# An attention block and a gated feed-forward layer on one core: another order of the loading phase, and the scores of the first two batches transposed together

## The chip, the cores and the metric

The kernel runs on one core of one Trainium2 chip. The time is the device time of one execution in microseconds (us); a run's time is compared with runs of the kernel before on the same chip. TensorE is called PE here, VectorE DVE, ScalarE ACT, GpSimd POOL, and SyncE, which only issues transfers here, SP.

## What is computed

```python
# x (8, 8, 512, 64), state (8, 8, 32, 64), both fp32; D = 64, scale = 1/8
scores  = scale * x @ state.T ;  a  = softmax(scores)   # 512 rows of 32
xread   = a @ state
scores2 = scale * state @ x.T ;  a2 = softmax(scores2)  # 32 rows of 512
sread   = a2 @ x
y = concat([xread, sread], axis=2)       # per batch 512 + 32 rows, 8 heads x 64 = 512 wide
gate = sigmoid(y @ w_gate);  val = y @ w_val            # 512 x 1536 each
out  = (gate * val) @ w_out                             # 1536 x 512 -> (4352, 512) fp32
```

## The kernel before

For the 512 x-rows of a batch, `xread @ W` is never formed from `xread`. The kernel first multiplies the state with both weight matrices (`sw_visit`, `sw_wide`: two PSUM tiles, one for each parity e of the head, copied to the SBUF tile `SW` by `sw_cp`), and then `SW` with the transposed probabilities `aT` (`gv_mm(b, f)`: four matmuls of 512 columns, two for the gate, two for the value, for block f of 12). ACT takes a tanh of the gate half (`gv_th`), DVE multiplies it with the value half (`gv_glu`), and `out_mm(b, k)` (four matmuls) is one third of one of four output tiles; after the last third ACT copies the tile (`res`) and SP writes it.

The probabilities of a batch b come from `S_mm` (halves i = 0, 1), `S_max` and `S_sub` (DVE), `S_exp` (ACT), `n_sum` (DVE, a reduction and a reciprocal), `n_mul` (POOL), and a transposition: `aT_mm` with `aT_cp` on PE, ACT and DVE for batches 0 and 1, `aT_dma` (SP) for the others. The second softmax, by columns, is `cT_mm` (scores transposed, one PSUM tile for each e), `cT_max` (DVE), `cT_exp` (ACT), `cT_nrm` (a reciprocal `rc` on DVE, then `cN` on POOL), `c_dma` (SP transposes), and `sr_mm` with `sr_cp` (the 32 rows of `sread`, put into `XS`). All eight batches' `XS` rows go through the feed-forward layer together as "batch 8" at the end.

The order on each engine is the order of the program's lines (`manual_schedule`): an instruction that waits holds up all that stand behind it on its engine. PSUM has eight tiles of one bank: two named GV, four SWP, one OU, one AT; the caller names the place. A tile can be used again when all that read its last content are through. SBUF pools have rings too; the one that matters is `cE` (output of `cT_exp`) with two buffers, which POOL's `cN` reads.

The program has three parts: a loading phase and prologue, written out as a list of calls (L423 to L694), in which batches 0 and 1 are computed as far as their weights have landed and batch 2 is prepared; a loop over b = 2 to 8 and f = 0 to 11 (L696), in which block f of batch b stands beside a third of an output tile of batch b - 1 and the preparation of batch b + 1 (`row`, `col`); and a tail. The second softmax of batches 0 and 1 is left to the stage b = 7, which prepares no batch. There `col(0, f)` runs in f = 0 to 4 and `col(1, f - 3)` in f = 3 to 7. In that stage the order in each f is a third of an output tile of batch 6, block f of batch 7, and then these steps.

Weights come by POOL's queue in column blocks of 256 or 512 (`load_w(w, lo, n)`, w = 0 gate, 1 value), x by SP's queue (batch 2's and 3's by POOL's), the state by both; `gate(...)` is a one-column POOL copy that makes POOL wait for something before it issues more. `warm(n, place)` is n small matmuls of ones whose result is not used; before and after have 87 of them in all.

Of the kernel before, what the change touches and what calls it, by code (L numbers as in the profile page):

```python
# [10 lines left out]
AF = mybir.ActivationFunctionType  # L11
# [5 lines left out]
def kernel(  # L17
# [14 lines left out]
    nc = tc.nc  # L32
# [311 lines left out]
    def warm(n, place):  # L344

        ps = place[0].tile((128, 512), FP, name="warm", tag=place[1])
        for _ in range(n):
            nc.tensor.matmul(ps[:, :128], ones[:, 0], ones[:, 0], start=True, stop=True)  # L348
# [36 lines left out]
    def col(b, t):  # L385
# [11 lines left out]
        else:  # L397
            cT_nrm(b, 1, nc.gpsimd)
            c_dma(b)

    def row(b, t):

        if t == 0:
            S_mm(b, 0, AT)
            S_max(b, 0)
        elif t == 1:
            S_sub(b, 0)
            S_mm(b, 1, SWP)
            S_max(b, 1)
        elif t == 2:  # L410
            S_sub(b, 1)
            S_exp(b, 0)
        elif t == 3:
            S_exp(b, 1)
            n_sum(b, 0)
            n_mul(b, 0, nc.gpsimd)
        elif t == 4:
            n_sum(b, 1)
            n_mul(b, 1, nc.gpsimd)
        else:  # L420
            aT_dma(b)
# [7 lines left out]
        nc.vector.memset(ones[:, e, 64 - e * 64:128 - e * 64], 0.0)  # L429
# [3 lines left out]
    warm(16, GV)  # L433
    warm(3, SWP)
    load_x(1, nc.sync, 4)
    warm(3, AT)
    cast_x(1, pool, 0, 2)
    xT_mm(1, 0, SWP)
    load_w(1, 0, 256)
    warm(15, OU)  # L440
    nc.scalar.activation(pre[:, 0:1], ones[:, 0, 0:1], AF.Exp)
    cast_s(0, pool)
    load_sb(1)
    load_w(0, 0, 256)
# [24 lines left out]
    S_mm(1, 1, GV)
    S_max(1, 1)  # L470
    cast_x(0, act, 2, 2)
    xT_mm(0, 1, OU)
    xT_mm(0, 2, AT)
    xT_cp(0, 1, act)
    S_sub(1, 1)
    xT_mm(0, 0, OU)
    xT_cp(0, 2, act)
    load_w(1, 512, 512)
    cast_x(0, pool, 6, 2)
    S_sub(1, 0)  # L480
    gate(xfs[0][:, 7, 0, 0:1])
    xT_cp(0, 0, vec)
    xT_mm(0, 3, GV)
    warm(8, SWP)
    load_sb(3)
    load_w(0, 512, 512)
    warm(4, GV)
    S_mm(0, 0, GV, (0,))
    S_mm(0, 0, AT, (1,))
    S_exp(1, 1)  # L490
    n_sum(1, 1)
    S_exp(1, 0)
    sw_visit(0, 0, 256)
    n_sum(1, 0)
    sw_visit(1, 0, 256)
    xT_cp(0, 3, act)
    sw_cp(0, 0, 2, 1, act)
    S_mm(0, 1, GV, (0,))
    S_mm(0, 1, OU, (1,))
    sw_cp(0, 0, 2, 0, act)  # L500
    n_mul(1, 1, nc.gpsimd)
    sw_cp(1, 0, 2, 0, act)
    S_max(0, 0)
    S_sub(0, 0)
    n_mul(1, 0, nc.gpsimd)
    aT_mm(1, AT)
    sw_visit(1, 256, 256)
    load_sb(2)
    sw_cp(1, 0, 2, 1, act)
# [12 lines left out]
    sw_cp(1, 256, 2, 1, act)
    gv_mm(1, 2, SWP)
    S_exp(0, 1)
    sw_cp(0, 256, 2, 1, vec)
    load_x(2, nc.gpsimd, 2)
    gv_th(1, 1)
    sw_visit(1, 512, 512, 1)
    gv_mm(1, 0, GV)
    gv_th(1, 2)  # L530
    gv_glu(1, 1)
    sT_cp(1, vec)
    sT_mm(3, OU)
    sw_cp(1, 512, 1, 1, act)
    n_sum(0, 1)
    sw_visit(1, 512, 512, 0)
    sw_cp(1, 512, 1, 0, act)
    gv_th(1, 0)
    sw_visit(0, 512, 512, 0)
    sT_cp(3, act)  # L540
    gv_glu(1, 2)
    load_w(0, 1024, 512)
    n_mul(0, 0, nc.gpsimd)
    sT_mm(2, AT)
    load_w(1, 1024, 512)
    sw_cp(1, 512, 0, 1, act)
    sw_cp(0, 512, 0, 0, act)
    n_mul(0, 1, nc.gpsimd)
    aT_mm(0, OU)
    sw_cp(1, 512, 0, 0, vec)  # L550
    aT_cp(0, 0, act)
    aT_cp(0, 1, act)
    gv_mm(1, 6, SWP)
    cast_x(2, pool, 0, 4)
    sw_visit(0, 512, 512, 1)
    gv_th(1, 6)
    sw_cp(0, 512, 1, 1, act)
    gv_mm(1, 5, GV)
    gv_th(1, 5)
    sw_cp(0, 512, 0, 1, vec)  # L560
    gv_glu(1, 0)
    gv_mm(0, 0, SWP)
    gv_th(0, 0)
    gv_glu(1, 6)
    cast_x(2, pool, 4, 4)
    sw_cp(0, 512, 1, 0, vec)
    gv_glu(0, 0)
    gv_mm(0, 5, SWP)
    gv_mm(1, 4, SWP)
    gv_th(1, 4)  # L570
    gv_mm(0, 2, GV)
    gv_th(0, 5)
    gv_th(0, 2)
    gv_glu(1, 5)
    gv_mm(0, 7, SWP)
    gv_glu(1, 4)
    sT_cp(2, act)
    gv_mm(0, 6, SWP)
    gv_th(0, 7)
# [24 lines left out]
    S_mm(2, 1, OU)
    gv_glu(0, 4)
    gv_th(0, 9)
    load_wo(1)
    gv_glu(0, 1)
    gv_glu(0, 8)
    load_wo(2)  # L610
    gate(glus[1][:, 4, 0:1])
    gv_glu(0, 9)
    S_max(2, 1)
    gv_mm(1, 3, SWP)
    gv_th(1, 3)
    gv_mm(0, 3, SWP)
    gv_th(0, 3)
    gv_glu(1, 3)
    S_sub(2, 1)
    load_x(3, nc.gpsimd)  # L620
    gv_glu(0, 3)
    gv_mm(0, 11, SWP)
    gv_th(0, 11)
    gv_glu(0, 11)
    gv_mm(0, 10, GV)
    gv_th(0, 10)
    gv_glu(0, 10)
    sw_wide(2, 0)
    S_exp(2, 1)
    out_mm(0, 1, GV)  # L630
    sw_cp(2, 0, 1, 0, act)
    sw_cp(2, 0, 2, 0, act)
    sw_cp(2, 0, 0, 1, vec)
    n_sum(2, 1)
# [24 lines left out]
    cT_exp(2, 1)
    sw_visit(1, 1024, 512, 0)  # L660
    sw_cp(1, 1024, 0, 1, vec)
    sw_cp(1, 1024, 0, 0, act)
    out_mm(0, 0, GV)
    sw_cp(2, 0, 0, 0, vec)
    out_mm(0, 11)
    gv_mm(1, 8, SWP)
    gv_th(1, 8)
    cT_max(2, 0)
    cT_exp(2, 0)
    gv_glu(1, 8)  # L670
    out_mm(0, 2)
    sw_wide(2, 1)
    sw_cp(2, 1, 0, 0, vec)
    sw_cp(2, 1, 1, 1, vec)
    at_xT_dma(3)
    load_x(4, nc.sync)
    sw_cp(2, 1, 1, 0, act)
    sw_cp(2, 1, 0, 1, act)
    out_mm(0, 10)
    gv_mm(1, 9, SWP)  # L680
    sw_cp(2, 1, 2, 0, act)
    gv_th(1, 9)
    gv_glu(1, 9)
    out_mm(0, 4)
    gv_mm(1, 11, SWP)
    gv_th(1, 11)
    sw_cp(2, 1, 2, 1, vec)
    gv_glu(1, 11)
    gv_mm(1, 10, GV)
    gv_th(1, 10)  # L690
    gv_glu(1, 10)
    cT_nrm(2, 0, nc.gpsimd)
    cT_nrm(2, 1, nc.gpsimd)
    c_dma(2)  # L694

    for b in range(2, B + 1):  # L696
        nb = b + 1 if b + 1 < B else None
        for f in range(NF):
# [14 lines left out]
            if nb is not None:  # L713
# [18 lines left out]
            if b < B and f == 9:  # L732
# [45 lines left out]
```

## Time and profile before

| | us |
|---|---|
| runs: median of three (231.16, 232.07, 232.13) | 232.07 |
| the profiled execution, its own time | 230.65 |
| its span from first to last instruction | 228.9 |
| PE busy | 219.1 |
| ACT busy, DVE busy, POOL busy | 143.1, 138.0, 71.4 |

The profile is one execution. Its span leaves out 1.75 us of the execution's own time, before and behind the instructions. In the answers, a line of the timeline has the start, the length (both us), the engine, the source line, the operation with output and input tile and shapes, how many such instructions the line merges, and in brackets the idle time before it with what ended it. PE's merged matmuls are pipelined and their ends are modelled, so starts are the safer figure. In the groups by line, the last columns are the busy time, the mean length of one in ns, and the idle time before. A row of the table of stretches has start, end and length, then busy time and count on PE, PE's weight loads, DVE, ACT and POOL, PE's granted clock, the DMA share and GB/s.

### The profile page before, as it was taken

The page shows a single profiled execution, that of the slowest core. Times are in us where ns is not written, and L with a number is a line of the kernel's source. Part 1 is how long each engine was busy: PE and PEld are TensorE (multiplying, and loading weights), DVE is VectorE, ACT ScalarE, POOL GpSimd, SP SyncE. Part 2 cuts the span into 40 slices and gives each one's busy share as a digit, 9 for nine tenths or more (in the row PEclk, how much of TensorE's full clock was granted, in tenths as well). Part 3 has the DMA queues.
Part 4 walks back from the last instruction along what each step waited for, and adds up shares of the span by engine and source line. Part 5 has one row for each costly group of instructions (what it writes and reads, how often), then busy time and mean ns, then how long its engine had stood idle before and what let it go on. Part 6 is the DMA issues. An engine that isn't in the chain of part 4 may idle for free.

```text
span 228.9 us, 5007 instructions
## 1 busy us (share of the span) xinstructions
PE 219.1 (96%) x1885; PEld 111.5 (49%) x1911; DVE 138.0 (60%) x266; ACT 143.1 (63%) x288; POOL 71.4 (31%) x77
## 2 busy tenths in 40 slices
PE   8868999999999999999999999999999999999994
PEld 7653444434444444444444444445444434566744
DVE  0889779766587557666766577648755664422311
ACT  3588787677575866676767767584857655422411
POOL 3986371240507080307130533031301355000001
PEclk9999999999999999999999999999999999999999
DMA  6999979935794374842443766313121312411114
GB/s 215 269 201 285 206 88 182 269 85 126 209 292 134 61 181 94 246 148 74 92 126 83 238 84 142 89 46 87 57 46 75 99 37 69 116 39 77 46 26 115
DMA packets 47271, 29.49 MB, mean 129 GB/s; under 512 B 29872, under 2 KB 42544, under 8 KB 47248
## 3 DMA queue, kind: packets, MB, share of 16 engines
q1 hardware_dynamic: 40096, 21.84, 36.5%
q0 software_dynamic: 6864, 7.14, 17.0%
q8 instruction: 15, 0.25, 0.4%
q10 hardware_dynamic: 288, 0.20, 0.3%
q14 instruction: 8, 0.07, 0.1%
HBM read 18.35 MB, written 8.91 MB: 119 GB/s over the span
## 4 chain that ended last, share of the span: by engine, by line
PE 84%; DMA 7%; ACT 2%; issue 2%; POOL 2%; SPq 1%; DVE 0%; ACTq 0%
PE outp L314 36%; PE gvp L283 34%; PE swp L231 5%; PE gvp L286 5%; DMA wg<-in_moe_w_gate_dram 4%; DMA xf<-in_x_dram 2%; PE srp L216 2%; PE Sp L121 1%; SPq L74 1%; PE outp L334 1%; PE cTp L181 1%; POOL cN L204 1%; ACT res L318 1%; POOL xb L91 1%; ACT SW L269 1%
## 5 line engine op out<-in xcount | busy, mean ns | idle before, releaser
L298 DVE SCALAR_TENSOR_TENSOR glu<-th,gvp 128x512 bf16<-128x512 f32 (+1 forms) x108 | 70.3, 656 | 69.1 <-ACT th L293 52.8
L314 PE MATMUL outp<-wo,glu 128*128 128x512 bf16 x370 | 95.5, 379 | 1.7 <-issue 0.3
L283 PE MATMUL gvp<-aT,SW 128*128 128x512 bf16 x384 | 96.6, 379 | 0.3 <-DVE aT L169 0.3
L293 ACT ACTIVATE th<-gvp 128x512 f32<-128x512 f32 (+1 forms) x108 | 61.8, 576 | 51.2 <-PE gvp L283 41.4
L283 PEld LDWEIGHTS <-SW 128*128 128x128 bf16 x384 | 36.3, 98 | 44.8 <-issue 3.1
L314 PEld LDWEIGHTS <-glu 128*128 128x128 bf16 x396 | 36.5, 98 | 40.8 <-issue 3.2
L204 POOL TENSOR_SCALAR cN<-cE,rc 128x512 bf16<-128x512 f32 x16 | 24.9, 1564 | 66.2 <-DVE rc L201 53.4
L269 ACT CAST SW<-swp 128x512 bf16<-128x512 f32 x74 | 41.0, 586 | 3.5 <-PE swp L231 2.5
L152 POOL TENSOR_TENSOR ab<-E,ri 128x512 bf16<-128x512 f32 x16 | 16.7, 1047 | 48.4 <-DVE ri L146 21.7
L318 ACT ACTIVATE res<-outp 128x512 f32<-128x512 f32 x33 | 19.7, 597 | 16.8 <-PE outp L314 16.6
L269 DVE CAST SW<-swp 128x512 bf16<-128x512 f32 x22 | 14.7, 681 | 1.0 <-PE swp L231 1.0
L91 POOL CAST xb<-xf 128x1024 bf16<-128x1024 f32 (+1 forms) x14 | 13.6, 986 | 4.9 <-DMA xf<-in_x_dram 4.9
L196 ACT ACTIVATE cE<-cTp,nb 128x512 f32<-128x512 f32 x16 | 11.1, 694 | 0.8 <-POOL cN L204 0.8
L144 DVE TENSOR_REDUCE rs<-E 128x16 f32<-128x512 f32 x16 | 10.8, 675 | 0.7 <-ACT E L137 0.7
L188 DVE TENSOR_REDUCE cm<-cTp 128x1 f32<-128x512 f32 x16 | 10.9, 682 | 0.4 <-PE cTp L181 0.4
L137 ACT ACTIVATE E<-E 128x512 f32<-128x512 f32 x16 | 10.1, 637 | 1.6 <-DVE E L134 1.6
L129 DVE TENSOR_REDUCE mx<-Sp 128x16 f32<-128x512 f32 x16 | 10.7, 674 | 0.4 <-PE Sp L121 0.4
L134 DVE TENSOR_TENSOR E<-Sp,mx 128x512 f32<-128x512 f32 x16 | 10.9, 684 | 0.1
L325 POOL DMA_DIRECT2D out_dram<-res x2 | 1.1, 550 | 30.1 <-ACT res L318 30.1
L231 PE MATMUL swp<-wg,sTc 64*32 64x512 bf16 (+1 forms) x192 | 8.4, 328 | 0.2
L348 PE MATMUL warm<-ones 128*128 128x128 bf16 x87 | 7.6, 256 | 1.0 <-DVE ones L429 1.0
L231 PEld LDWEIGHTS <-sTc 64*32 64x32 bf16 x384 | 4.8, 91 | 7.4 <-issue 4.7
(62 smaller groups left out, 134.2 us busy)
## 6 DMA issues: line engine op xcount, KB each, us to landing
out_dram<-res SPq DMA_DIRECT2D x31, 256.0 KB, 2.4
xf<-in_x_dram SPq DMA_DIRECT2D x12, 256.0 KB, 4.8
xf<-in_x_dram SPq DMA_DIRECT2D x3, 1024.0 KB, 6.3
wo<-in_moe_w_out_dram POOLq DMA_DIRECT2D x3, 512.0 KB, 8.9
wv<-in_moe_w_val_dram POOLq DMA_DIRECT2D x2, 512.0 KB, 9.1
wg<-in_moe_w_gate_dram POOLq DMA_DIRECT2D x2, 512.0 KB, 10.1
xf<-in_x_dram POOLq DMA_DIRECT2D x2, 512.0 KB, 8.0
xf<-in_x_dram POOLq DMA_DIRECT2D x1, 1024.0 KB, 12.8
```

Source lines behind the costliest of these rows:

```text
L91: cp(xbs[b].rearrange("p c h d -> p h c d")[:, lo:lo + n], xfs[b][:, lo:lo + n])
L152: eng.tensor_tensor(abs_[b].rearrange("p c e (j n) -> p (c e) j n", n=Ns)[:, ce, 2 * i:2 * i + 2], halfE(b, i)[:, ce], ri[:, ce].unsqueeze ...
L196: nc.scalar.activation(ex, held["cT", b][e], AF.Exp, bias=held["nb", b, e], scale=scale, accum_out=cs)
L204: eng.tensor_scalar(held["cN", b][:, e], held["cE", b, e], rc, None, op0=ALU.mult)
L231: nc.tensor.matmul(pss[e][j * Ns:(j + 1) * Ns, o:o + n], sTc[rows, b, j] if b > 1 else sTz[rows, b, j, e], (wg, wv)[w][rows, j, lo:lo + n] ...
L269: cp(*sw_left.pop((b, lo, w, e)))
L283: nc.tensor.matmul(ps, SWs[b][:, g, w, fs], aTs[b][:, :, g], start=(g == 0), stop=(g == 1))
L286: nc.tensor.matmul(ps, (wg, wv)[w][:, j, fs], XS[:, j], start=(j == 0), stop=(j == 3))
L293: nc.scalar.activation(th, held["gv", b, f][0], AF.Tanh, scale=0.5)
L298: nc.vector.scalar_tensor_tensor(glus[b][:, f], held["th", b, f], 1.0, held["gv", b, f][1], ALU.add, ALU.mult)
L314: nc.tensor.matmul(ops[b, c], glus[b][:, f, c * 128:(c + 1) * 128], wo[:, f], start=(f == 0), stop=(f == NF - 1))
L318: nc.scalar.activation(res, ops[b, c], AF.Copy, scale=0.5)
```

## The change

The list of the loading phase and prologue is in another order; what is computed is the same. The order of POOL's weight loads is value 256:512, gate 256:512, gate 0:256, value 0:256 (before: value 0:256, gate 0:256, gate 256:512, value 256:512), then the blocks of 512 as before, of the last two the value first. So the first blocks of columns that batch 1 works on are f = 2 and 3. `load_x(0)` stands later in the list, but SP still issues the eight parts of batch 1 and batch 0 one behind the other from the start, since nothing on SP stands between them. Some steps change engines: up to the main loop five `sw_cp`, one `sT_pad`, one `aT_cp`, one `sT_cp`, one `cast_x` of two heads and one `n_mul` more are on DVE, and two `xT_cp` and one `cast_x` of four heads fewer. In the stage b = 7, `first01` takes the place of `col(0, ...)` and `col(1, ...)`.

```diff
+    def sr_all(b, place):
+        sr_mm(b, place)
+        sr_cp(b, 0, act)
+        sr_cp(b, 1, vec)
+
+    def first01(f):
+        if f == 0:
+            for k in range(2):
+                cT_mm(k, (SWP, SWP))
+            cT_max(0, 0)
+        elif f == 1:
+            cT_max(0, 1)
+            cT_exp(0, 0)
+        elif f == 2:
+            cT_max(1, 0)
+        elif f == 3:
+            cT_max(1, 1)
+            cT_exp(0, 1)
+            cT_nrm(0, 0, nc.gpsimd)
+        elif f == 4:
+            cT_exp(1, 0)
+            cT_nrm(0, 1, nc.gpsimd)
+        elif f == 5:
+            sr_all(B - 1, AT)
+        elif f == 6:
+            c_dma(0)
+            cT_exp(1, 1)
+            cT_nrm(1, 0, nc.gpsimd)
+        elif f == 7:
+            cT_nrm(1, 1, nc.gpsimd)
+            c_dma(1)
+        elif f in (9, 11):
+            sr_all(f // 2 - 4, AT)
...
             if b == B - 1:
-                if f == 10:
-                    sr_cp(b, 0, act)
-                    sr_cp(b, 1, vec)
-                for k in range(2):
-                    if 0 <= f - 3 * k < 5:
-                        col(k, f - 3 * k)
-                    elif f == 8 + 3 * k:
-                        sr_mm(k, SWP)
-                        sr_cp(k, 0, act)
-                        sr_cp(k, 1, vec)
+                first01(f)
```

Of the new list, the places that the prediction speaks of (`...` where lines are left out):

```python
    cast_x(1, vec, 6, 2)
    ...
    cast_x(0, vec, 0, 2)
    ...
    S_max(1, 0)                      # DVE: S_sub(1, 0), S_max(1, 1), S_sub(1, 1), S_max(0, 0),
    ...                              # n_sum(1, 0), S_sub(0, 0), n_sum(1, 1), n_sum(0, 0)
    sw_visit(1, 256, 256)
    sw_cp(1, 256, 2, 1, act)
    sw_visit(0, 256, 256)
    sw_cp(1, 256, 2, 0, act)
    sw_cp(0, 256, 2, 1, act)
    ...
    aT_mm(1, OU)
    aT_cp(1, 0, act)
    ...
    aT_cp(1, 1, vec)
    gv_mm(1, 2, GV)
    ...
    gv_mm(0, 11, GV)
    S_mm(2, 1, SWP)                  # before: S_mm(2, 1, OU)
    ...
    gv_mm(0, 9, SWP)
    S_max(2, 1)
    gv_th(0, 9)
    gv_glu(0, 9)
    gv_mm(0, 10, GV)
    gv_th(0, 10)
    S_sub(2, 1)
    sw_wide(2, 0)
    ...
    cT_mm(2, (SWP, SWP))
    out_mm(0, 3)
    n_sum(2, 0)
    n_mul(2, 0, nc.vector)
    ...
    sw_visit(1, 1024, 512, 0)
    sw_cp(1, 1024, 1, 0, vec)
    ...
    out_mm(0, 4)
    ...
    out_mm(0, 11)
    ...
    sw_cp(1, 1024, 0, 1, vec)
    sw_cp(1, 1024, 0, 0, vec)
    gv_mm(1, 9, SWP)
    ...
    sw_wide(2, 1)
```

More of the change, by code (lines that the diff above doesn't have):

```diff
@@ L474 @@
[L474 to L484, printed above, removed]
+    warm(6, AT)
+    load_x(1, nc.sync, 4)
+    nc.vector.memset(sTz, 0.0)
+    warm(15, GV)
+    nc.scalar.activation(pre[:, 0:1], ones[:, 0, 0:1], AF.Exp)
+    warm(8, AT)
+    cast_s(0, pool)
+    sT_mm(0, GV)
+    sT_pad(0, 0, vec)
+    cast_x(1, pool, 0, 2)
@@ L488 @@
-    S_mm(0, 0, GV, (0,))
-    S_mm(0, 0, AT, (1,))
-    S_exp(1, 1)
-    n_sum(1, 1)
[L492 to L497, printed above, removed]
+    n_sum(1, 0)
+    xT_cp(0, 3, act)
+    n_mul(1, 0, nc.gpsimd)
+    xT_cp(0, 2, act)
+    S_sub(0, 0)
+    sT_cp(1, act)
+    n_sum(1, 1)
+    warm(8, OU)
+    n_mul(1, 1, nc.gpsimd)
+    S_exp(0, 0)
+    n_sum(0, 0)
+    n_mul(0, 0, nc.gpsimd)
     S_mm(0, 1, GV, (0,))
     S_mm(0, 1, OU, (1,))
-    sw_cp(0, 0, 2, 0, act)
@@ L523 @@
[L523 to L526, printed above, removed]
+    gv_glu(1, 2)
+    sw_cp(0, 0, 2, 1, act)
+    sw_visit(0, 512, 512, 1)
+    gv_th(1, 0)
+    load_w(1, 1024, 512)
+    n_sum(0, 1)
+    n_mul(0, 1, nc.gpsimd)
+    gv_mm(1, 3, SWP)
+    aT_mm(0, OU)
     gv_th(1, 1)
+    gv_glu(1, 0)
     sw_visit(1, 512, 512, 1)
-    gv_mm(1, 0, GV)
-    gv_th(1, 2)
+    sT_mm(3, AT)
+    sw_cp(0, 512, 1, 0, vec)
+    gv_th(1, 3)
+    gv_glu(1, 3)
+    aT_cp(0, 1, vec)
@@ L543 @@
[L543 to L546, printed above, removed]
-    sw_cp(0, 512, 0, 0, act)
[L548 to L552, printed above, removed]
+    sw_cp(1, 512, 0, 1, vec)
+    cast_x(2, pool, 4, 4)
+    at_xT_dma(2)
+    sT_cp(2, vec)
+    gv_mm(1, 7, SWP)
+    gv_th(0, 3)
+    sw_visit(0, 512, 512, 0)
+    gv_glu(0, 3)
+    gv_th(1, 7)
+    sw_cp(0, 512, 0, 0, act)
+    gv_mm(1, 4, GV)
@@ L553 @@
+    gv_mm(0, 2, SWP)
+    sw_cp(0, 512, 0, 1, vec)
+    gv_th(0, 2)
+    gate(xfs[0][:, 7, 0, 0:1])
+    gv_glu(1, 7)
+    gv_th(1, 4)
+    gv_glu(0, 2)
+    gv_glu(1, 4)
     gv_mm(1, 6, SWP)
[L554 to L555 removed]
     gv_th(1, 6)
[L557 to L567 removed]
@@ L612 @@
[L612 to L622, printed above, removed]
     gv_th(0, 11)
     gv_glu(0, 11)
+    gv_mm(0, 9, SWP)
+    S_max(2, 1)
+    gv_th(0, 9)
+    gv_glu(0, 9)
     gv_mm(0, 10, GV)
     gv_th(0, 10)
+    S_sub(2, 1)
+    sw_wide(2, 0)
+    load_x(3, nc.gpsimd)
+    S_mm(2, 0, GV)
     gv_glu(0, 10)
-    sw_wide(2, 0)
+    out_mm(0, 1, OU)
@@ L664 @@
-    sw_cp(2, 0, 0, 0, vec)
-    out_mm(0, 11)
-    gv_mm(1, 8, SWP)
+    sw_cp(2, 0, 2, 1, act)
+    S_sub(2, 0)
+    sw_visit(1, 1024, 512, 1)
+    S_exp(2, 0)
+    cT_mm(2, (SWP, SWP))
+    out_mm(0, 3)
+    n_sum(2, 0)
+    n_mul(2, 0, nc.vector)
+    n_mul(2, 1, nc.gpsimd)
+    aT_dma(2)
+    cT_max(2, 0)
+    sw_cp(2, 0, 2, 0, act)
+    cast_x(3, pool, 4, 4)
+    sw_cp(1, 1024, 1, 1, vec)
+    cT_max(2, 1)
+    cT_exp(2, 0)
+    cT_exp(2, 1)
+    out_mm(0, 6, GV)
+    cT_nrm(2, 0, nc.gpsimd)
@@ L667 @@
+    gv_mm(1, 8, SWP)
+    gate(xTs[2][:, 0, 3, 0:1])
+    gv_mm(1, 11, SWP)
     gv_th(1, 8)
-    cT_max(2, 0)
-    cT_exp(2, 0)
+    sw_cp(2, 1, 2, 0, vec)
+    sw_cp(2, 1, 0, 1, vec)
     gv_glu(1, 8)
[L671 to L684, printed above, removed]
```

264 lines of the change are left out of this document (126 added, 138 removed).

## The prediction

> **What bounds the kernel now.** I read the page first, then the table of stretches, then the timeline of the loading phase and of the stage b = 7.
>
> ```profile
> span 228.9 us, 5007 instructions
> PE 219.1 (96%) x1885; PEld 111.5 (49%) x1911; DVE 138.0 (60%) x266; ACT 143.1 (63%) x288; POOL 71.4 (31%) x77
> PE 84%; DMA 7%; ACT 2%; issue 2%; POOL 2%; SPq 1%; DVE 0%; ACTq 0%
> ...
> 10.00:15.00 5.00, 3.34 (x78) 2.65 (x76) 4.86 (x11) 4.28 (x10) 4.11 (x7) 1.00 1.41 196
> 25.00:30.00 5.00, 5.00 (x24) 2.25 (x23) 3.83 (x7) 3.82 (x9) 1.04 (x1) 1.00 1.28 151
> ...
> 24.89 7.08 PE L283 MATMUL gvp<-aT,SW 128*128 128x512 bf16 x32
> 40.52 1.04 PE L314 MATMUL outp<-wo,glu 128*128 128x512 bf16 x3
> 56.66 0.41 PE L231 MATMUL swp<-wg,sTc 64*32 64x512 bf16 x8
> ```
>
> PE bounds it (84% of the chain). From 24.89 us it has no gap to speak of: eight blocks follow each other (32 matmuls in 7.08 us; in steady pace a block or an output step takes 0.86, half of 184.82 to 186.54 in the rows of b = 7 below), the first output matmul starts at 40.52, and the main loop's first `sw_wide` at 56.66. Before that PE is short of work, and DVE is the busiest engine (4.86 of 5 us from 10 to 15). So a gain can come only from filling PE earlier than 24.89, and a loss from any gap opened later. Behind 57 the loop is the same until the stage b = 7. I cost three parts: loading, the rest of the prologue, and that stage.
>
> **Loading: does batch 1's lead arrive?** The rows of before, and x batch 0's first part (issued at 2.77, landed 5.1 us later):
>
> ```profile
> 2.77 0.48 SPq L74
> xf<-in_x_dram SPq DMA_DIRECT2D x1, 256.0 KB, 5.1
> ...
> 9.53 1.29 DVE L129 TENSOR_REDUCE mx<-Sp 128x16 f32<-128x512 f32 x2 [0.41 <-PE Sp L121]
> 10.85 1.29 DVE L134 TENSOR_TENSOR E<-Sp,mx 128x512 f32<-128x512 f32 x2
> 12.39 0.67 DVE L144 TENSOR_REDUCE rs<-E 128x16 f32<-128x512 f32 x1
> 13.10 0.25 DVE L146 RECIPROCAL ri<-rs 128x16 f32<-128x16 f32 x1
> 13.51 2.05 POOL L152 TENSOR_TENSOR ab<-E,ri 128x512 bf16<-128x512 f32 x2 [0.89 <-DVE ri L146]
> 13.51 2.05 ACT L269 CAST SW<-swp 128x512 bf16<-128x512 f32 x4 [0.23 <-PE swp L231]
> 16.27 0.59 ACT L169 COPY aT<-aTp 128x512 bf16<-128x512 bf16 x1 [0.71 <-PE aTp L159]
> 16.89 0.42 DVE L169 COPY aT<-aTp 128x512 bf16<-128x512 bf16 x1 [0.84 <-ACT aT L169]
> 17.37 1.21 PE L283 MATMUL gvp<-aT,SW 128*128 128x512 bf16 x4 [0.33 <-DVE aT L169]
> ```
>
> In the new order DVE casts x batch 0's first part before `S_max(1, 0)`. It lands at 2.77 + 5.1 = 7.87, the cast takes some 0.46, so `S_max(1, 0)` starts at 8.4, 1.1 us earlier than the 9.53 of before. Then DVE does `S_max` and `S_sub` of both halves of batch 1 (4 x 0.65, to 11.0), and then, ahead of batch 1's second sum, `S_max(0, 0)` (0.65), `n_sum(1, 0)` (0.86 to the next start), `S_sub(0, 0)` (0.65) and `n_sum(1, 1)` (0.67 and 0.25, 0.96 from start to end). That is 14.1, and 14.3 with 0.2 for `S_mm(0, 0)`, which PE finishes at about 11.2. POOL's `n_mul(1, 1)` starts 0.16 later and takes 1.03: 15.5, against 13.51 + 2.05 = 15.56. The lead is spent on batch 0. Then ACT: by the same count it ends `xT_cp(0, 2)` at 13.5, and PE comes, behind 8 `warm`, `S_mm(0, 1)` and 2 more, to the first `sw_visit` at 14.5; three `sw_cp` (2.05 / 4 = 0.51 each) run from 14.97 to 16.5 ahead of `aT_cp(1, 0)`. With 0.59 and 0.42 behind them the first block starts at 17.6, 0.25 later than 17.37.
>
> From there DVE sets the pace:
>
> ```profile
> L298 DVE SCALAR_TENSOR_TENSOR glu<-th,gvp 128x512 bf16<-128x512 f32 x24 | 15.8, 681 | 5.5 <-ACT th L293 5.3
> L269 DVE CAST SW<-swp 128x512 bf16<-128x512 f32 x12 | 7.9, 680 | 1.0 <-PE swp L231 1.0
> 28.75 3.28 DVE L298 SCALAR_TENSOR_TENSOR glu<-th,gvp 128x512 bf16<-128x512 f32 x5 [0.44 <-ACT th L293]
> ```
>
> The change puts five more `sw_cp` on DVE before the main loop (5 x 0.68 = 3.4), and with the small copies, casts and one `n_mul` some 4.4 us more in all. From 8.4 to its tenth `gv_glu` the new list gives DVE four `S_max` and four `S_sub` (8 x 0.65), four `n_sum` (4 x 0.86), six `sw_cp`, two `aT_cp` and two `sT_cp` (4 x 0.42, the `aT` row) and ten `gv_glu` (16 x 0.68): 21.2 us, so it cannot be done before 29.6. In the trace of before the tenth is the fourth of the run of five that starts at 28.75, and ends at 28.75 + 4 x 0.656 = 31.4. So loading may gain up to 1.8 if DVE never waits. Following the new list by hand with these lengths I find 2.5 us of waits on it, the largest of 1.0 at block (0, 3): its tanh stands on ACT behind `aT_cp(0, 0)` and three `sw_cp`, and `aT_mm(0)` runs only at 22.4. The tenth then ends at 32.1, 0.7 late. I take **+0.5**, bounds -1.8 and +0.7: the hand count is nearer, but each step in it has a rounding of some 0.05.
>
> Loads issued later: POOL now does `n_mul(0, 0)` (1.03) before `load_sb(2)` and x batch 2, and by the count the last weight block is issued at 22.4.
>
> ```profile
> wg<-in_moe_w_gate_dram POOLq DMA_DIRECT2D x2, 512.0 KB, 10.1
> 31.67 2.30 POOL L85 DMA_DIRECT2D wo<-in_moe_w_out_dram x3
> DMA to landing us min/median/max: 7.2/8.9/10.8
> ```
>
> With 10.1 us to landing that block is there at 32.5, and `sw_visit(0, 1024, 512, 0)` comes to it at about 34.4: nothing. `load_wo` stands behind `pad`, which waits for `sT_cp(3)`, now on DVE behind the ninth `gv_glu`: it is issued at 33.1 instead of 31.67 and lands (7.2) at 40.3, before its use at 41.9; at the 10.8 of the third it would be 43.9. I take nothing; that end is a rival.
>
> **The clock.** The `warm` matmuls are spread differently: 29 in a row at the start, then groups of 16, 13, 12, 8.
>
> ```profile
> 1.01 3.81 PE L348 MATMUL warm<-ones 128*128 128x128 bf16 x34 [1.01 <-DVE ones L429]
> 5.26 1.56 PE L348 MATMUL warm<-ones 128*128 128x128 bf16 x25
> 22.21 0.67 PE L231 MATMUL swp<-wg,sTz 64*32 64x512 bf16 x16 [0.56 <-DMA wg<-in_moe_w_gate_dram]
> ```
>
> The first 34 took 112 ns each, the next 25 took 62, and the pace stayed although PE was busy only 3.34 of 5 us from 10 to 15, with gaps like that of 0.56. My count of the new order has no gap above 0.7, so I add nothing. The Trainium skill (TensorE: Matmul & The Clock Gate, section "Part 1: The HAM clock gate") has the array start at half clock and fall back to it after an idle window, 3.4 us by its figure; the two paces agree with the first half of that, though the profile's granted clock reads 1.00 throughout, and no trace here shows a fall-back.
>
> **The rest of the prologue.** In before, 24.89 to 56.66 has no loss: any wait is new. I find three. (a) `S_mm(2, 1)` moves from OU to an SWP tile, and `sw_wide(2, 0)` needs all four SWP tiles, so its last pair waits for `S_sub(2, 1)`. With T the start of block (0, 10), DVE does `S_max(2, 1)`, `gv_glu(0, 9)`, `S_sub(2, 1)` from T on, 3 x 0.66 = 2.0, and PE is there at T + 0.86 + 0.65 = T + 1.5: +0.5. (b) `gv_mm(1, 9)` follows `sw_visit(1, 1024, 512, 0)` after only two output steps and needs copies that are now DVE's. Behind `cT_mm(2)` DVE has `n_mul` (0.7 to 1.05, between its own and POOL's price), two `cT_max` (0.83 each), two `rc` (0.16), four `sw_cp` (2.7): 5.3; PE has five output steps and a visit, 4.7: +0.5 or so. (c) `sw_wide(2, 1)` waits for `gv_glu(1, 9)`, up to +0.5. Bounds 0 (DVE ahead of my count) and +1.5; I take **+1.0**.
>
> **The stage b = 7.**
>
> ```profile
> 177.98 0.41 PE L181 MATMUL cTp<-xT,sTz 64*32 64x512 bf16 x8
> 178.32 1.04 PE L314 MATMUL outp<-wo,glu 128*128 128x512 bf16 x4
> 184.57 0.15 DVE L201 RECIPROCAL rc<-cs 128x1 f32<-128x1 f32 x1
> 184.64 0.67 DVE L188 TENSOR_REDUCE cm<-cTp 128x1 f32<-128x512 f32 x1
> 184.82 1.03 PE L283 MATMUL gvp<-aT,SW 128*128 128x512 bf16 x4
> 184.88 1.56 POOL L204 TENSOR_SCALAR cN<-cE,rc 128x512 bf16<-128x512 f32 x1 [5.52 <-ACT th L293]
> 186.48 0.69 ACT L196 ACTIVATE cE<-cTp,nb 128x512 f32<-128x512 f32 x1 [0.37 <-POOL cN L204]
> 186.54 1.03 PE L283 MATMUL gvp<-aT,SW 128*128 128x512 bf16 x4
> 187.16 0.59 ACT L318 ACTIVATE res<-outp 128x512 f32<-128x512 f32 x1
> 187.80 1.02 PE L314 MATMUL outp<-wo,glu 128*128 128x512 bf16 x4 [0.23 <-ACT res L318]
> 192.97 0.63 PE L216 MATMUL srp<-Eb,xb 128*128 128x64 bf16 x16
> 193.44 1.03 PE L314 MATMUL outp<-wo,glu 128*128 128x512 bf16 x3
> ```
>
> Read it as one chain: `cT_exp(1, 0)` on ACT (186.48) waits for POOL's `cN(0, 0)` (184.88 to 186.44), whose `cE` buffer it takes; `res` (187.16) stands behind it on ACT, and the OU tile of f = 6 (187.80) waits for `res`. Block f = 5, started at 186.54, was through 0.86 later, at 187.40: 0.4 us of PE is lost. The change merges the two transpositions: a visit alone holds PE for 178.32 less 177.98, 0.34; eight matmuls straight behind another eight add, as an estimate, the time of one, 0.86 / 4 = 0.22, so 0.12 or a little more is saved. But `cT_nrm(0, 0)` keeps its f = 3, now behind `cT_max(1, 1)` (0.67 and 0.15, with small gaps 0.9) on DVE, where before `rc` at 184.57 stood ahead of the reduction at 184.64; and all of it is 0.22 later since the second visit now stands ahead. `cN(0, 0)` then starts at 184.88 + 0.9 + 0.22 = 186.0, ends at 187.56, and the step f = 6 starts at 187.80 + 1.12 = 188.92. Into that wait falls `sr_mm(7)`, moved from f = 9 (192.97 to 193.44, 0.47). Net **+0.65**; bounds -0.2 (no wait at all) and +1.1. Behind it nothing is late: the last `cN` ends at about 195.4, its transposes land before `sr_mm(1)` at 199.8.
>
> **Sum.** 0.5 + 1.0 + 0.65 = +2.15 us on the profiled execution: 230.65 + 2.15 = 232.8, span 231.05. The runs' median, 232.07, lies 1.4 above that execution, so the forecast for the median is **234.2**.
>
> **Rivals.** *DVE never waits*: the 1.1 us lead is carried on, loading gains 1.8, the middle loses nothing, the end 0.65: -1.15, 230.9, and 230.0 if ACT is not held in f = 4 either. For it: the lower bound of the count. Against: DVE must then be busy without a gap for 21 us, and in before it waits on `th` for 5.3 us over this phase. Chance 0.12. *It evens out*: loading -0.5, no new waits, end +0.65: 232.2, chance 0.18. *The first block of `wo` is late*: if it takes over 8.8 us (41.9 less 33.1) to land, output steps wait up to 2.0: 236.2, chance 0.08. *The clock falls once*: 34 matmuls at the slow pace took 3.81, so such a stretch loses half, 1.9: 236.1, chance 0.02. *The change does not do what it says*: x batch 0 is issued as before, so "batch 1 ahead" is DVE's and PE's order alone; that is in the forecast.
>
> **Numbers.** The forecast has 0.60, with its own range 233 to 235.6. The range 231.2 to 236.0 leaves out most of the first rival and the tails above. A measurement here can tell about 0.5%, 1.16 us: faster by more 0.12, within 0.18, slower by more 0.70 (0.60 + 0.08 + 0.02).
>
> **What would show it.** Right: a first block at 17.4 to 17.8, the tenth `gv_glu` ending after 31.4, a wait of `swp` on DVE just before the first output step, the main loop starting at 57.5 to 59, and an `outp` wait on ACT `res` of 1 us or more in the stage b = 7. Wrong: PE without gaps from before 24 us, or the main loop starting before 56.

## The result, and the profile after

The changed kernel takes 231.89 us (median of 22 runs, 230.84 to 233.06), the kernel before 231.18 in the same runs (230.37 to 232.25). The ratio is 1.0035, 95% interval 1.002 to 1.0049: 0.7 to 0.8 us slower. The forecast was 234.2, 2.1 us over a kernel before taken at 232.07; a third of the 2.1 came, and 0.9 of the 2.3 us between 234.2 and 231.89 is the base, since the median of the first three runs lay that much above the median of 22. The profiled execution of the changed kernel took 231.08 us with a span of 229.2, against 230.65 and 228.9: the traces account for 0.3 to 0.4 us, and the experiments look for the rest.

The head of the page of the changed kernel:

```profile
span 229.2 us, 5034 instructions
...
PE 220.7 (96%) x1911; PEld 110.7 (48%) x1911; DVE 141.9 (62%) x273; ACT 141.1 (62%) x282; POOL 69.9 (30%) x76
...
PE 87%; ACT 5%; DVE 2%; DMA 2%; issue 1%; POOL 1%; SPq 0%; ACTq 0%
```

PE bounds it as before, and DVE has 3.9 us more work. The timeline of PE, at the places that answer to those of the prediction:

```profile
16.76 3.10 PE L283 MATMUL gvp<-aT,SW 128*128 128x512 bf16 x12 [0.55 <-DVE aT L169]
...
25.52 4.49 PE L283 MATMUL gvp<-aT,SW 128*128 128x512 bf16 x20
...
39.27 0.27 PE L231 MATMUL swp<-wg,sTc 64*32 64x256 bf16 x1
39.71 0.30 PE L231 MATMUL swp<-wg,sTc 64*32 64x256 bf16 x7 [0.17 <-DVE E L134]
...
40.30 4.48 PE L314 MATMUL outp<-wo,glu 128*128 128x512 bf16 x20
...
50.23 1.04 PE L283 MATMUL gvp<-aT,SW 128*128 128x512 bf16 x4
...
56.40 0.41 PE L231 MATMUL swp<-wg,sTc 64*32 64x512 bf16 x8
...
186.91 0.63 PE L216 MATMUL srp<-Eb,xb 128*128 128x64 bf16 x16
...
188.60 1.02 PE L314 MATMUL outp<-wo,glu 128*128 128x512 bf16 x4 [1.06 <-ACT res L318]
...
200.95 0.60 PE L286 MATMUL gvp<-XS,wg 128*128 128x256 bf16 x4
```

The first block starts at 16.76 (17.37 before). The seventh starts at 25.52; in the kernel before it is the third of the run at 24.89, and 24.89 + 2 x 0.865 = 26.62, so the lead has grown to 1.1 us. Most of it is gone at the first output step (40.30 against 40.52), and the main loop starts 0.26 early (56.40 against 56.66). Behind that the changed kernel loses: 1.06 us at the output step f = 6 of the stage b = 7, and batch 8 begins 0.34 late (200.95 against 200.61).

### The profile page after: what moved, and what is told of

It is laid out like the page before. It is cut to its first block, busy times and chain, and to the rows that moved or that the text cites. A ratio compares the mean times of both kernels' runs of the same rounds, so it can differ in the third digit from the quotient of the medians.

```text
span 229.2 us, 5034 instructions
## 1 busy us (share of the span) xinstructions
PE 220.7 (96%) x1911; PEld 110.7 (48%) x1911; DVE 141.9 (62%) x273; ACT 141.1 (62%) x282; POOL 69.9 (30%) x76
## 4 chain that ended last, share of the span: by engine, by line
PE 87%; ACT 5%; DVE 2%; DMA 2%; issue 1%; POOL 1%; SPq 0%; ACTq 0%
PE outp L314 37%; PE gvp L283 35%; PE swp L231 5%; PE gvp L286 5%; DMA xf<-in_x_dram 2%; PE Sp L121 2%; PE srp L216 1%; ACT SW L269 1%; PE outp L334 1%; PE cTp L181 1%; ACT xT L108 1%; ACT E L137 1%; DVE glu L298 1%; PE warm L348 1%; ACT th L293 1%
## 5 line engine op out<-in xcount | busy, mean ns | idle before, releaser
L314 PE MATMUL outp<-wo,glu 128*128 128x512 bf16 x396 | 98.6, 379 | 1.1 <-ACT res L318 1.1
L269 ACT CAST SW<-swp 128x512 bf16<-128x512 f32 x69 | 38.6, 585 | 3.9 <-PE swp L231 2.7
L152 POOL TENSOR_TENSOR ab<-E,ri 128x512 bf16<-128x512 f32 x15 | 15.7, 1051 | 55.5 <-DVE ri L146 26.1
L269 DVE CAST SW<-swp 128x512 bf16<-128x512 f32 x27 | 17.9, 680 | 0.4 <-PE swp L231 0.4
L91 POOL CAST xb<-xf 128x1024 bf16<-128x1024 f32 (+1 forms) x14 | 13.0, 946 | 6.2 <-DMA xf<-in_x_dram 6.2
```

Source lines behind the costliest of these rows:

```text
L91: cp(xbs[b].rearrange("p c h d -> p h c d")[:, lo:lo + n], xfs[b][:, lo:lo + n])
L152: eng.tensor_tensor(abs_[b].rearrange("p c e (j n) -> p (c e) j n", n=Ns)[:, ce, 2 * i:2 * i + 2], halfE(b, i)[:, ce], ri[:, ce].unsqueeze ...
L269: cp(*sw_left.pop((b, lo, w, e)))
L314: nc.tensor.matmul(ops[b, c], glus[b][:, f, c * 128:(c + 1) * 128], wo[:, f], start=(f == 0), stop=(f == NF - 1))
```

## Experiments

Each kernel ran in 5 rounds beside the kernel before, whose median was 230.85 in the rounds of the first four kernels, 230.91 in those of the next four (value early, `wo` early, both, the gap filled), 230.95 in those of the three with more or fewer `warm` and the moved copies, and 230.65 in those of the last. Ratios and differences are to the kernel before in the same rounds.

**The end.** Two kernels take one half of the change each, two more the same halves with the steps of the end in another order. The end of the change alone, behind the loading list of the kernel before:

```
...
             if b == B - 1:
...
+                first01(f)
```

> The loading list of the kernel before with the changed end (first01, both transpositions in one visit). Theory A (the end is the loss: rc(0,0) stands behind cT_max(1,1), so POOL's first cN is late, cT_exp(1,0) waits on ACT for its cE buffer and holds res): +0.6 us against the kernel before (0.3%), the output step f = 6 of the stage b = 7 waits about 1 us for ACT res, and from the first block of that stage to the first block of batch 8 it takes 25.9 us in place of 25.3. Rival B (the loss of the changed kernel is in its loading, in executions other than the profiled one): within 0.2 us of the kernel before.

Measured: 231.42, ratio 1.0019 (1.0000 to 1.0038), +0.57 us.

The loading list of the change alone, with the end of the kernel before:

```
-                first01(f)
...
+                for k in range(2):
+                    if 0 <= f - 3 * k < 5:
+                        col(k, f - 3 * k)
...
```

> The changed loading list with the end of the kernel before. Theory A: 0.3 us faster than the kernel before (231.2 - 0.3 = 230.9), as the main loop starts at 56.4 in place of 56.7 and everything behind it is as before. Rival B: its median is 0.2 to 0.6 us slower than the kernel before, since the changed kernel's median lies 0.8 us above the one before and the profiled executions account for only 0.34 of it; the loading would then differ from one execution to the next, and the main loop start at 56.4 to 57.3.

Measured: 230.82, ratio 1.0007 (0.9981 to 1.0032): no difference that can be told, though the profiled execution started its main loop at 56.36 as expected.

The changed kernel with the end reordered:

```
         elif f == 2:
+            cT_nrm(0, 0, nc.gpsimd)
+            cT_exp(0, 1)
             cT_max(1, 0)
         elif f == 3:
+            cT_nrm(0, 1, nc.gpsimd)
             cT_max(1, 1)
-            cT_exp(0, 1)
-            cT_nrm(0, 0, nc.gpsimd)
         elif f == 4:
             cT_exp(1, 0)
-            cT_nrm(0, 1, nc.gpsimd)
         elif f == 5:
             sr_all(B - 1, AT)
+            cT_exp(1, 1)
...
```

> The changed kernel with the steps of its end in another order: cT_nrm(0,0) and cT_exp(0,1) at f = 2, cT_nrm(0,1) at f = 3, so that POOL's cN(0,0) starts behind cT_exp(0,0) and not behind cT_max(1,1); cT_exp(1,1) at f = 5. The merged visit and the early sr of batch 7 stay. Theory A: no wait for ACT res at f = 6; the stage takes 24.7 us in place of 25.9, so 1.2 us faster than the changed kernel, 230.7. If the hold on ACT is not the cause, and the merged visit or the early sr is, it stays at 231.9.

Measured: 230.70, ratio 0.9979 (0.9959 to 0.9998), 0.15 us under the kernel before, where the changed kernel lay 0.71 over it. Its median is 1.2 us below that of the changed kernel, but the kernel before was 0.33 faster in these rounds too, so that 0.9 is the fairer figure.

The same end behind the loading list of the kernel before:

> The loading list of the kernel before with the reordered end of the kernel above. Theory A: the 0.4 us wait of the kernel before at f = 6 goes and 0.12 is saved by the merged visit: 0.6 us faster than the kernel before, 230.6. If the loading is neutral it equals the kernel above; if the changed loading gains 0.3, the kernel above is 0.3 faster; if it costs 0.5 in most executions, this one is 0.5 faster.

Measured: 230.11, ratio 0.9966 (0.9948 to 0.9984), 0.74 us under the kernel before, and 0.6 under the changed list with the same end, in the same rounds.

The time from the last `sw_wide` of the main loop to the first block of batch 8 is the same for each end, whatever the loading (rows of the timeline of PE: the kernel before, then the loading list of the change with the old end and with the reordered one):

```profile
164.10 0.41 PE L231 MATMUL swp<-wg,sTc 64*32 64x512 bf16 x8
...
200.61 0.60 PE L286 MATMUL gvp<-XS,wg 128*128 128x256 bf16 x4
```

```profile
163.80 0.41 PE L231 MATMUL swp<-wg,sTc 64*32 64x512 bf16 x8
...
200.31 0.60 PE L286 MATMUL gvp<-XS,wg 128*128 128x256 bf16 x4
```

```profile
163.74 0.41 PE L231 MATMUL swp<-wg,sTc 64*32 64x512 bf16 x8
...
187.28 1.03 PE L314 MATMUL outp<-wo,glu 128*128 128x512 bf16 x4
...
199.63 0.60 PE L286 MATMUL gvp<-XS,wg 128*128 128x256 bf16 x4
```

That is 36.51 with the old end, behind either loading list, and 35.89 with the reordered one (35.90 behind the old list). The changed kernel has 37.12, the end alone 37.11. So the change's end costs 0.61 and reordering it gains 1.22. The chain stands in the timelines of DVE, POOL and ACT of the changed kernel:

```profile
184.52 0.68 DVE L188 TENSOR_REDUCE cm<-cTp 128x1 f32<-128x512 f32 x1
...
185.38 0.15 DVE L201 RECIPROCAL rc<-cs 128x1 f32<-128x1 f32 x1
...
185.69 3.10 POOL L204 TENSOR_SCALAR cN<-cE,rc 128x512 bf16<-128x512 f32 x2 [6.60 <-ACT th L293]
...
187.29 0.69 ACT L196 ACTIVATE cE<-cTp,nb 128x512 f32<-128x512 f32 x1 [1.68 <-POOL cN L204]
...
187.97 0.59 ACT L318 ACTIVATE res<-outp 128x512 f32<-128x512 f32 x1
```

`rc` stands behind the fourth reduction (184.52), POOL starts its first `cN` at 185.69, and ACT waits 1.68 us for the `cE` buffer with `res` behind it. In the reordered kernel POOL starts both `cN` of batch 0 earlier, `cT_exp(1, 0)` (185.41) does not wait, and the step f = 6 follows `sr_mm(7)` at 187.28 without a wait:

```profile
183.01 1.56 POOL L204 TENSOR_SCALAR cN<-cE,rc 128x512 bf16<-128x512 f32 x1 [4.01 <-ACT cE L196]
...
184.75 1.56 POOL L204 TENSOR_SCALAR cN<-cE,rc 128x512 bf16<-128x512 f32 x1 [0.18 <-DVE rc L201]
...
185.41 0.68 ACT L196 ACTIVATE cE<-cTp,nb 128x512 f32<-128x512 f32 x1
```

**The loading, which differs from one execution to the next.** With the reordered end the changed list gave 229.70 to 229.78 in five executions and 230.67 to 231.37 in seven, all with a mean granted clock of 0.998 to 1.0. A late load was the first suspect. First the last of the early weight blocks, issued sooner:

```
     load_w(0, 0, 256)
+    load_w(1, 0, 256)
...
-    load_w(1, 0, 256)
     load_w(1, 512, 512)
```

> The changed loading list with the reordered end, and load_w(1, 0, 256) issued right behind load_w(0, 0, 256), at about 7.8 us in place of 9.6 to 10.0. In the traces of the changed list this block lands 5.7 to 6.5 us after its issue, at 15.7 to 15.9, and the visit that needs it starts its second matmuls at 15.7 to 16.0: no margin, where the kernel before had 8.2 us between issue and use. Theory C (in the executions that are 1 us longer, this block lands later): the executions at 230.7 to 231.4 go, the median falls to 229.7. If another wait makes them long, they stay, median 230.6.

Measured: 230.44, ratio 0.9981 (0.9961 to 1.0001); six executions of twelve still lie at 230.69 to 231.56. Theory C, that this block comes late in the long executions, falls. Then the blocks of `wo`:

```
     sT_cp(2, vec)
+    sT_cp(3, vec)
...
-    sT_cp(3, vec)
```

> The changed loading list with the reordered end, and sT_cp(3) on DVE right behind sT_cp(2), so that pad and the three blocks of wo can be issued some 3 us earlier (28.5 in place of 31.5). Rival D (in the longer executions a block of wo lands late; its third block lands at 42.7 to 43.7 in the traces and is used at 43.7): the executions at 230.7 to 231.4 go, the median falls to 229.7. By theory C they stay and the median is 230.6.

Measured: 237.13, ratio 1.0265 (1.0241 to 1.029). Every execution is long for a new reason, so this run cannot tell whether `wo` was late in the long ones (the trace of a long one, below, does). Issued at 28.73 in place of 31.57, the blocks of `wo`, and x of batch 3 right behind them, meet the transposing DMAs of xT(2) on their way, and `S_mm(2, 1)` waits for those:

```profile
26.77 5.36 SPq L113 DMA_TRANSPOSE xT<-xb  x4
...
28.73 2.23 POOL L85 DMA_DIRECT2D wo<-in_moe_w_out_dram  x3
...
43.63 0.32 PE L121 MATMUL Sp<-sTz,xT 128*128 128x64 bf16 x5 [2.99 <-DMA xT<-xb]
```

The time from issue to landing of the four transposing DMAs, here and below it in the changed kernel, where they were issued at 26.09:

```profile
DMA to landing us min/median/max: 5.4/8.9/12.9
```

```profile
DMA to landing us min/median/max: 3.6/4.0/4.4
```

In the changed kernel the late issue of `wo` keeps them apart.

> Both edits together. By C or D 229.7; if each explains a part of the longer executions, only this one has all its executions at 229.7 to 230.0. If the long executions come from neither, about half of them stay at 230.7.

Measured: 237.12, ratio 1.0269 (1.0245 to 1.0293), with the same wait (4.7 us for xT in its trace). It tells nothing beyond the run before it.

**PE's pace at the start.** The profiled execution of the kernel with the early weight block happened to be one of the long ones (first block at 17.93, main loop at 57.56, 1.2 us later than in the changed kernel). Its timeline of PE, and below it that of the changed kernel:

```profile
1.02 3.27 PE L348 MATMUL warm<-ones 128*128 128x128 bf16 x29 [1.02 <-DVE ones L464]
...
4.73 1.30 PE L105 MATMUL xTp<-ident,xb 128*128 128x128 bf16 x8
...
6.82 1.91 PE L348 MATMUL warm<-ones 128*128 128x128 bf16 x16
...
10.88 0.89 PE L348 MATMUL warm<-ones 128*128 128x128 bf16 x13
```

```profile
1.02 3.13 PE L348 MATMUL warm<-ones 128*128 128x128 bf16 x29 [1.02 <-DVE ones L464]
...
4.64 0.40 PE L105 MATMUL xTp<-ident,xb 128*128 128x128 bf16 x4 [0.24 <-POOL xb L91]
...
6.59 1.06 PE L348 MATMUL warm<-ones 128*128 128x128 bf16 x16
```

The same 16 `warm` took 1.91 us in the one and 1.06 in the other. No load was late here: DVE casts the parts of x at 5.88 and 7.20, against 5.87 and 7.13. PE ran at half pace until some 10 us, the transposes and `S_mm` before the first maximum took longer, and `S_max(1, 0)` started at 9.20 in place of 8.06. From the first block to the main loop this execution takes 39.63 us, the changed kernel 39.64, so neither `wo` nor anything else behind the first block made it long: rival D falls here. In the traces of this list the pace changes between 3.9 and 6.3 us in four kernels, at 10.3 in this one and at about 13 in the one with the early `wo`. The profile's granted clock reads 1.00 in these stretches of all of them. The test is to give PE more `warm`, and fewer:

```
     sT_mm(0, GV)
+    warm(12, AT)
```

> The changed loading list with the reordered end, and 12 more warm matmuls behind sT_mm(0), ahead of the first transposes. Theory F: the executions that are about 1 us longer come from PE's pace at the start. The changed list has 29 warm in a row (the kernel before 34, then 25 more) and then waits for x; in one trace the switch from 107 to 54 ns for each came only at 10.3 us, in others at 4.1 to 6, and the slow one has all that follows 1.2 us later, without any late load. With 12 more (1.3 us at the slow pace) the matmuls run on until 5.5 us: the long executions go, nearly all lie at 229.7 to 230.0, median 229.8. If the pace at the start is not the cause (theory C, a late weight block, or another load), half of them stay at 230.7.

Measured: 230.04, ratio 0.9964 (0.9941 to 0.9987); ten executions of twelve at 229.66 to 230.46, one of 230.72, one of 232.28 at a clock of 0.992. In its trace the pace changes before the first transpose at 5.48.

```
-    warm(6, AT)
     load_x(1, nc.sync, 4)
...
-    warm(15, GV)
+    warm(8, GV)
...
-    warm(8, AT)
```

> The changed loading list with the reordered end, and 8 warm matmuls at the start in place of 29. Theory F: PE switches late in every execution, at 7 to 13 us, so there are none at 229.7 and the median is 230.9 or more. If the warm matmuls are only filling, it is as with 29 (230.4 to 230.7, some at 229.7).

Measured: 231.77, ratio 1.0027 (1.0007 to 1.0047), none under 230.54. Its trace:

```profile
1.02 1.03 PE L348 MATMUL warm<-ones 128*128 128x128 bf16 x8 [1.02 <-DVE ones L464]
...
7.56 1.91 PE L348 MATMUL warm<-ones 128*128 128x128 bf16 x16
...
11.66 0.89 PE L348 MATMUL warm<-ones 128*128 128x128 bf16 x13
...
18.84 3.10 PE L283 MATMUL gvp<-aT,SW 128*128 128x512 bf16 x12 [0.54 <-DVE aT L169]
...
58.48 0.41 PE L231 MATMUL swp<-wg,sTc 64*32 64x512 bf16 x8
```

The pace doubles at about 11.3, the main loop starts at 58.48. Theory F, that the long executions come from PE's pace at the start, stands in its main part: 8 matmuls that compute nothing at the start and 41 of them lie 1.7 us apart by the median, in the same rounds. It is not the whole: a part of x can land late too. In the trace with 8 `warm` DVE waits for one until 6.43 (5.87 in the changed kernel), and in that of the kernel with the moved copies, below, for another until 7.75 (7.13), although its pace had changed before 6 us; its first block comes at 17.52, against 17.00 with the same 41 `warm`:

```profile
6.43 0.67 DVE L91 CAST xb<-xf 128x512 bf16<-128x512 f32 x1 [1.59 <-DMA xf<-in_x_dram]
```

```profile
7.75 0.43 DVE L91 CAST xb<-xf 128x512 bf16<-128x512 f32 x1 [0.85 <-DMA xf<-in_x_dram]
```

How many of the long executions each of the two makes is not known, since only one execution of each kernel has a trace. What the traces do show is where the difference lies: in the eight of this list without the early `wo` the first block starts anywhere from 16.67 to 18.84, and from there to the main loop it is 39.63 or 39.64 us in every one. The kernel before takes 39.29.

Last, the changed kernel itself with 12 more `warm`:

> The changed kernel, its end as it is, with 12 more warm matmuls behind sT_mm(0). The changed kernel lies at 231.89 (0.35% over the kernel before). By theory A plus F: the kernel with the reordered end and the same 12 warm lies at 230.04, and the end as it is takes 144.55 us from the start of the main loop to the first block of batch 8 in place of 143.33, so 230.04 + 1.22 = 231.26, some 0.3 us over the kernel before. If the warm matmuls do nothing here it stays at 231.9; if the end does not add up with the loading it is below 231.0.

Measured: 231.17, ratio 1.003 (1.0013 to 1.0046), 0.52 us over the kernel before in the same runs. The time is near the expected 231.26, and six of its nine executions lie at or under 231.2, against five of 22 without the `warm`. But the kernel before was also 0.5 faster in these rounds, and the ratio cannot be told from the 1.0035 of the changed kernel: that the parts add up is likely, not shown. For the end they do: this kernel and the one with the reordered end and the same `warm` lie 0.52 over and 0.91 under the kernel before, 1.43 apart, where the traces have 1.22.

**The gap of the kernel before.** With the old loading list the traces of the end alone and of the reordered end show something that the profile of before did not: the clock falls. The table of stretches of the end alone (start and end, then the busy time of PE, PEld, DVE, ACT and POOL, the granted clock, the DMA share and GB/s), and a row of its timeline of PE:

```profile
13.00:15.00 2.00, 1.29 (x48) 0.91 (x47) 1.93 (x5) 1.76 (x5) 1.19 (x2) 1.00 1.40 195
15.00:17.00 2.00, 1.08 (x16) 0.89 (x24) 1.32 (x3) 0.88 (x3) 2.00 (x3) 0.72 1.26 206
17.00:20.00 3.00, 3.00 (x51) 1.53 (x44) 2.29 (x5) 3.00 (x6) 1.68 (x3) 0.62 1.27 207
```

```profile
15.91 1.03 PE L159 MATMUL aTp<-ident,ab 128*128 128x128 bf16 x8 [1.62 <-POOL ab L152]
```

After the 1.62 us without matmuls the granted clock is 0.72 and then 0.62, and the eight transposes take 1.03 us in place of 0.62. The trace of the reordered end behind this list has the same gap and a like fall (0.73, then 0.61). The gap alone does not make it, though: the trace of the kernel before has it too, with PE busy for only 1.00 of the 2 us from 13 to 15, and its clock reads 1.00 from there to 20 us:

```profile
15.62 0.62 PE L159 MATMUL aTp<-ident,ab 128*128 128x128 bf16 x8 [1.62 <-POOL ab L152]
```

From these transposes to the main loop it is 41.46 and 41.32 us with the fall and 41.04 without, so a fall costs 0.3 to 0.4. About half of the executions of this list show it in their mean clock (0.991 to 0.993). Filling the gap:

```
+    warm(20, AT)
     aT_mm(1, AT)
```

> The loading list of the kernel before with the reordered end, and 20 warm matmuls (20 x 0.062 = 1.2 us) ahead of aT_mm(1), in the 1.6 us in which PE waits for POOL's ab. In two traces of this list the granted clock is 0.61 to 0.73 from 15.9 to 19.8 us, and half of its executions show a mean clock of 0.991 to 0.993; the changed list has no such gap and shows it in 3 of 46. Theory E (the clock falls for lack of matmuls from 13 to 16 us): no execution under 0.998, the median falls from 230.1 to 229.8. If the gap is not what lowers the clock, half of the executions stay at 0.992 and the median at 230.1.

Measured: 230.03, ratio 0.9963 (0.9944 to 0.9983). Four of twelve still show a clock of 0.993 or less (two of them at 234.6 and 237.0, for which I have no cause). Fewer than half, and a median 0.08 lower; in its trace PE also waits 1.38 us for a weight block ahead of the filling. This is inconclusive.

**Does DVE set the pace?** Three of the copies that the change gave to DVE, put on ACT, in the kernel with 12 more `warm`:

```
-    sw_cp(0, 512, 0, 1, vec)
+    sw_cp(0, 512, 0, 1, act)
...
-    sw_cp(0, 1024, 1, 0, vec)
+    sw_cp(0, 1024, 1, 0, act)
...
-    sw_cp(0, 1024, 0, 1, vec)
+    sw_cp(0, 1024, 0, 1, act)
```

> The kernel with 12 more warm, and three of the copies sw_cp that the change put on DVE, those of sw_visit(0, 512, 512, 0) and of both visits of (0, 1024, 512), on ACT. By the prediction (DVE sets the pace of the loading phase and each such copy costs it 0.6 to 0.68) the main loop starts up to 1 us earlier and the median falls by as much. By the trace of the changed kernel PE has no gap from 23.3 us on and DVE waits for ACT's th before most of its gv_glu, so moving them gains nothing: within 0.3 of the kernel with 12 more warm, later if ACT's th are pushed back.

Measured: 230.31, ratio 0.9972 (0.9956 to 0.9987), 0.27 over the kernel it is to be compared with: no gain. The traces say it more sharply, since they leave out the start: from the first block to the main loop it is 39.64 us here (17.52 to 57.16) and 39.63 there (17.00 to 56.63). DVE does not set the pace of these steps.

## Why the prediction was wrong

**Loading: the step that failed.** Forecast +0.5; the seventh block is 1.1 us earlier than before. The first block, worked out as 17.6, started at 16.76. The working took the tenth `gv_glu` for the measure, at 32.1 against 31.4. It ended at 30.45. The timeline of DVE of the changed kernel:

```profile
8.06 0.68 DVE L129 TENSOR_REDUCE mx<-Sp 128x16 f32<-128x512 f32 x1
...
18.42 0.68 DVE L298 SCALAR_TENSOR_TENSOR glu<-th,gvp 128x512 bf16<-128x512 f32 x1
19.02 0.68 DVE L144 TENSOR_REDUCE rs<-E 128x16 f32<-128x512 f32 x1
...
21.41 0.69 DVE L298 SCALAR_TENSOR_TENSOR glu<-th,gvp 128x512 bf16<-128x512 f32 x1 [0.22 <-ACT th L293]
...
25.05 0.69 DVE L298 SCALAR_TENSOR_TENSOR glu<-th,gvp 128x512 bf16<-128x512 f32 x1 [1.08 <-ACT th L293]
...
27.65 1.88 DVE L298 SCALAR_TENSOR_TENSOR glu<-th,gvp 128x512 bf16<-128x512 f32 x3 [0.68 <-ACT th L293]
...
29.79 1.27 DVE L298 SCALAR_TENSOR_TENSOR glu<-th,gvp 128x512 bf16<-128x512 f32 x2
```

The waits were sized rightly: 2.5 us by hand, and here 0.49 (for `aT_cp(1, 0)`, at 16.29), 0.22, 1.08 (at block (0, 3), where the forecast had 1.0) and 0.68. Two other terms were not. `S_max(1, 0)` started at 8.06, not 8.4; this varies with when x lands (8.29 and 8.81 in two other traces with an early change of pace). And the work was put at 21.2 us, while from 8.06 to 30.45 less the waits it is 19.9: an instruction of 0.68 is followed by the next 0.60 after its start (18.42 and 19.02), and I had added lengths where starts count. 0.34 and 1.3 make the 1.65 us. The larger fault is the sentence "From there DVE sets the pace": from 23.3 us PE has no gap but 0.44 us at 39.27 and 0.2 ahead of 50.23, DVE waits for `th` (1.08 and 0.68 in the rows above), and taking three copies from it changed nothing (39.64 and 39.63). PE's own work set the pace there. Counting on DVE also missed what PE no longer does between the first and the seventh block: the kernel before waits there 0.56 us for a weight block (22.21) and runs six `warm`, the changed one does neither.

**The rest of the prologue.** Forecast +1.0; from the seventh block to the main loop the changed kernel takes 0.84 us longer (30.88 against 30.04). Wait (a) came as worked out, 0.44 us between 39.27 and 39.71. Waits (b) and (c) together cost some 0.2, not 1.0: block (1, 9) starts at 50.23 without a wait worth a mark, just behind DVE's last copy. The other 0.2 lies between the seventh block and 39, where I expected nothing; 0.13 of it is that the kernel before makes the two `sw_visit` of the last columns of batch 0 one right behind the other (31.90 to 32.45, 0.55 us), where the changed one makes them apart (0.34 us each).

**The stage b = 7.** Forecast +0.65, measured 0.61, by the chain that was described: `cN(0, 0)` at 185.69 (186.0 forecast, with the stage starting 0.27 earlier), the step f = 6 at 188.60 (188.92 forecast) behind a wait of 1.06 for `res`, with `sr_mm(7)` in front of it. This part was right in its mechanism too.

**The sum.** By the traces -1.10 + 0.84 + 0.61 = +0.35, against +2.15. Cut at the first block in place of the seventh, the loading list gains 0.61 ahead of it and loses 0.35 behind it. The medians lie 0.7 apart, 0.4 more than the traces. The likely reason is PE's pace at the start, which the forecast put at nothing because it asked only whether a gap would make the pace fall: "My count of the new order has no gap above 0.7, so I add nothing". It did not ask when the pace is first reached, with 29 matmuls in a row where the kernel before has 34 and soon 25 more. In all four traces of the old list those 25 run at 60 to 66 ns each from start to start, so that its pace had changed by 6 us. That the count of `warm` matters is shown with the reordered end (230.04 and 231.77); that it makes the 0.4 of the changed kernel is not, since with 12 more `warm` its ratio hardly moved, and late parts of x and the falls of the clock in the kernel before also shift the medians.

The Trainium skill (TensorE: Matmul & The Clock Gate, section "Part 1: The HAM clock gate") says that the window is free-running and that the same kernel switches at different points from run to run. The switches seen here agree with that in kind; the 500 ns that the Trainium skill gives there for the spread, with matmuls back to back, is far less than the 3.9 to 13 us here, where the matmuls have gaps. The Trainium skill, on the same page, section "HAM oscillation — how this bites in real kernels", gives as the rule to have no idle gaps over some 3.4 us; here a gap of 1.62 us was followed by a granted clock of 0.62 in two traces and by no fall in a third, so neither that rule nor the length of the gap alone decides. The Trainium skill, in Part 1 of that page, puts the cost of the start at under 1% of a typical span. Here a late change of pace costs 1.2 us of 229, 0.5%, which agrees, and it is more than the net of everything else in this change, 0.35 us by the traces.

**The rivals.** "It evens out" came nearest (232.2, with a gain in loading and +0.65 at the end), in part by luck: it had no new waits in the middle, and its base was 0.9 too high. "DVE never waits" had the loading gain but not its cause, for DVE did wait 2.5 us. In the trace of the changed kernel no output step waited for `wo`.

## What to carry over

Where PE starts at half pace, count the matmuls that run before its pace doubles as part of the order: the loading list that was 0.3 us faster in the traces where PE switched early was 0.6 slower than the old one by the medians (230.70 and 230.11, with the same end), and 12 idle matmuls only brought it level. Add up an engine's work by the distance of the starts, not by the lengths, and ask first whether that engine or PE is the one without gaps. In a chain of small steps across DVE, POOL and ACT, a two-instruction step that moves behind one reduction can hold the evictions of another loop; putting the two `cT_nrm` of batch 0 one step behind their `cT_exp`, with two `cT_exp` moved ahead, made the end faster behind both loading lists (by 0.61 us against the old end). With the reordered end the old list takes 230.11 and the changed list with 12 more `warm` 230.04, both about 0.35% under the kernel before.

## What was not expected of the hardware

PE's pace at the start is not settled by the kernel alone: with one order on PE up to there the 128x128 matmuls went from 107 ns (16 in the 1.71 us from 6.82 to 8.53) to 56 (16 in the 0.89 from 6.59 to 7.48) at about 4 us in one execution and at 10 or 13 in others, while the granted clock read 1.00. Transposing DMAs that landed in 3.6 to 4.4 us took 5.4 to 12.9 when the 1.5 MB of `wo`, with x of batch 3 behind it, were issued 2 us behind the first of them, and not 5.5 us.
